# Attention and mixture of experts in one kernel: ranks in pieces, overflow tables among the second parts, late sign adds, sums and searches on VectorE

## The chip, the cores and the metric

The kernel runs on one core of one Trainium2 chip. A core has five engines with instruction streams of their own: TensorE (PE in the profile; PEld is its weight load), VectorE (DVE), ScalarE (ACT), GpSimd (POOL) and SyncE (SP, which here issues DMA transfers). Each works through its stream strictly in order and waits on semaphores for what other engines produce. The metric is the device time of one execution in microseconds (us).

## What is computed

Eight batches of eight heads attend over 576 tokens with 64 features a head; of each row of scores only the 32 largest are kept. The result, 4608 tokens of 512 features, goes through a mixture of eight experts, of which each token takes the one with the largest logit:

```python
scores = scale * np.matmul(q, k.transpose(0, 1, 3, 2))
kth = np.partition(scores, -top_k, axis=-1)[..., -top_k:-top_k + 1]
scores = np.where(scores >= kth, scores, -1000000000.0)
attn = softmax(scores); attn_out = np.matmul(attn, v)
...
logits = x @ w_gate
expert_idx = np.argmax(logits, axis=1)
for e in range(E):
    xe = x[expert_idx == e]
    h = np.maximum(xe @ w1[e], 0.0)
    out[expert_idx == e] = gate_w[expert_idx == e, None] * (h @ w2[e])
```

## The kernel before

**Attention.** A loop `for t in range(steps + LAG + TD + 2)` runs 144 steps and some trailing turns. A step handles two tiles of 128 queries by 576 keys. TensorE makes the scores (`scores`), ACT copies them to `sb`, VectorE searches the 32nd largest value of each row with MAX8 and MATCH_REPLACE (`topk`; its last entries make `nb`, the threshold). `softmax` lets ACT write the sign of score minus threshold to `sg`, and POOL adds it: `sb <- sb + sg`, so that what lies below the threshold falls far down. Then come nine transposes on TensorE (`transp`, tile `tt`), the Exp on ACT (`exps`, tile `et`) and the product with v (`av`, tile `px`). The softmax's two tiles are handled one after the other, and `nb` of the last tile waits in POOL's stream behind the first tile's add.

**Side jobs.** Besides these fixed lines there are generators, one for each kind of further work: `j_sums` (sums of the softmax), `j_rows` (scaling to `xm`, the logits), `j_find` (finds the rows where the number of values at the threshold isn't right, and writes keys `r_lw`, `r_key`), `j_redo` (does such rows again, with their own search over `r_sb`, and subtracts `r_wk` on POOL), `j_patch` (their Exp transposes, their product `r_xa`, stored to `xs`), `j_route` (positions `pos` in the table of tokens by expert; indirect writes to `table`). A job yields `need(pool=1.2, act=0.8)` and the like: what it wants to spend in this step. `advance` lets it go on if the step's budget holds; after the steps `drain` lets all of them go on by one piece for each MoE round, without a limit. What a job queues with `pe`, `act`, `vec`, `pool` is issued by `flush` at fixed places of the step.

**MoE.** `moe()` is a generator of 128 rounds k, each one eighth of an expert's features: `hidden(k)` (tile `ph`; ACT makes `hh`, VectorE the rest `hl`), `project(k - 1)` (tile `y`, from `hh`, `hl`), `load_w(k + 3)` on SP, `split_w(k + 2)` (each weight tile `r` is split into a high part `wh` and a low part `wl`, the second `wl` on POOL once no job is left, on VectorE before), and now and then `fetch` (load of `ids`, indirect gather `gx` of the tokens) and `turn_x` (transposes `mt`, high and low parts `xh`, `xl`). The first 64 rounds are first parts: 256 tokens of each expert, by number. The rounds from 64 on are second parts, where the experts are taken by the number of their tokens, so that unequal widths are compiled in. `j_ahead` gathers the first expert's tokens to `kt` while attention still runs.

**Ranks and overflow.** Which expert stands in which second part is known only from the counts of tokens. After the drain the program, in written order, takes `counts` from the histogram, checks `lost`, clears the ends of the `hh`/`hl` tiles, and calls `ranks` (VectorE: keys, a comparison of all with all, `rank`, `base`, and `rtab`, the table that SP reads for the second parts' weights and ids) and `over` (cumulated overflow tiles, `te` and `tr`, for experts with more tokens than the second parts hold). `over` calls `step()`, which runs one MoE round, between its pieces. The first second part's ids and weights are fetched from round 54 on, when `late["on"]` is there.

Of the kernel before, what the change touches and what calls it, by code (L numbers as in the profile page):

```python
# [8 lines left out]
F32 = mybir.dt.float32  # L9
F32R = mybir.dt.float32r  # L10
# [4 lines left out]
OP = mybir.AluOpType  # L15
# [16 lines left out]
LAG = 2  # L32
# [9 lines left out]
VALS = TOPK + EXTRA  # L42
T0 = V0 + VALS + 1
# [11 lines left out]
def attention_moe(ctx, tc, q, k, v, w_gate, w1, w2, out):  # L55
    nc = tc.nc
    B, H, S, D = q.shape
    HP = H // 2
    DM = H * D
    E = w_gate.shape[1]  # L60
# [6 lines left out]
    DC, FC = DM // 128, F // 128  # L67
# [65 lines left out]
    ones = consts.tile([128, 128], BF, name="ones")  # L133
# [39 lines left out]
    SG = []  # L173
# [111 lines left out]
    def need(**k):  # L285
        return k
# [142 lines left out]

    def topk(t, us):  # L430
# [26 lines left out]
        def second(i):  # L457
# [21 lines left out]
                  (nc.gpsimd.tensor_tensor, (nb, v[:, :, 0:T0 + 1:T0], factors, OP.mult)),  # L479
                  (nc.gpsimd.tensor_tensor, (nb[:, :, 1], nb[:, :, 1], after, OP.subtract))]  # L480
# [56 lines left out]
    def j_sums(n):  # L537
# [3 lines left out]
        b = n // 2  # L541
# [5 lines left out]
        pool(nc.gpsimd.tensor_tensor, both, both, nm.to_broadcast([128, 2, NT, 8 + VALS]), op=OP.add)  # L547
        pool(nc.gpsimd.tensor_scalar, w, nm, -1.0, shift(b)[:, 1:2], op0=OP.mult, op1=OP.add)
        pool(nc.gpsimd.tensor_scalar, w, w, -1.25 * FAR, 1.25 * FAR, op0=OP.max, op1=OP.min)
# [8 lines left out]
        pool(nc.gpsimd.tensor_tensor, sums, sums, less, op=OP.subtract)  # L558
        pool(nc.gpsimd.tensor_scalar, sums, sums, 1e-9, None, op0=OP.add)
        pool(nc.gpsimd.tensor_tensor, sums, sums, w, op=OP.mult)  # L560
# [196 lines left out]
    def j_redo(p):  # L757
# [28 lines left out]
        pool(nc.gpsimd.tensor_tensor, sb, sb, dr, op=OP.subtract)  # L786
        act(nc.scalar.activation, sb, sb, AF.Exp, bias=nb[:, 0:1], scale=0.125, accum_out=nb[:, 1:2])
        start("patch", j_patch(p, sb, nb, qi, hmb), 4 * NT * (p + 1) + DUE['patch'])

    def j_patch(p, ex, nb, qi, hmb):  # L790
# [27 lines left out]
        pool(nc.gpsimd.tensor_tensor, xa, xa, hmb, op=OP.mult)  # L818
# [256 lines left out]
    def j_ahead():  # L1075
# [209 lines left out]
    ring = [0]  # L1285
# [38 lines left out]
    def moe():  # L1324
# [11 lines left out]
        for k in range(NU * FC):  # L1336
            u, f = divmod(k, FC)
# [30 lines left out]
    def ranks(sb, counts):  # L1368
# [13 lines left out]
        nc.vector.tensor_reduce(base, both, axis=AX.X, op=OP.add)  # L1382
        nc.vector.tensor_tensor(both, more, eight[:, :, None].to_broadcast([128, E, E]), op=OP.mult)
# [5 lines left out]
    def over(sb, counts, base, otab, step=lambda: None):  # L1389
# [189 lines left out]
    pc = ps_a.tile([128, E], F32, name="mt")  # L1579
    lost = moe_a.tile([128, B], F32, name="lost")  # L1580
# [8 lines left out]
    late["h"] = [[late["sb"].tile([128, 512], F32R, name=f"{n}{i}") for n in ("hh", "hl")] for i in range(2)]
    for x in late["h"]:  # L1590
        for y in x:
            nc.vector.memset(y.bitcast(F32)[:, WIDE:], 0.0)
# [52 lines left out]
```

## Time and profile before

| | |
|---|---|
| median of 3 runs | 1209.81 us (1208.26 to 1212.22) |
| profiled execution, its own time | 1202.35 us |
| its span in the trace | 1200.5 us |
| mean granted clock of TensorE, of full speed | 0.985 |
| busy time PE / DVE / POOL / ACT | 1134.9 / 985.5 / 827.0 / 814.1 us |

Steps fill the trace up to about 690 us, first parts of the MoE run from 713 to about 930, second parts after that. How to read rows of the trace: start in us, duration in us, engine, line of the kernel, operation, out<-in by the program's names, size, and in square brackets the idle time of the engine before it with the engine, tile and line that ended it. An engine with short idle times near the span's length is the bound; of the others idle time is no loss.

### The profile page before, as it was taken

The numbers are of one execution on the slowest core, as the hardware profiler recorded it, in microseconds if no ns is written. First come the engines' busy times: TensorE is split into PE (matmuls) and PEld (weight loads), VectorE is DVE, ScalarE is ACT, GpSimd is POOL, SyncE is SP. The second block draws the span as 40 slices with busy tenths as digits, with TensorE's granted clock in tenths as the row PEclk, the third lists the DMA queues.
The fourth block names the chain that finished last, engine by engine and source line by source line (L and its number), as shares of the span: only waits on it lengthen the run. The fifth ranks groups of instructions, "written<-read, shape, count | busy, mean of one in ns | idle before, by whom it ended". The sixth has DMA issues, their size and how long they took to land. (4 is left out here: it accounts for less than half of the span.)

```text
span 1200.5 us, 32495 instructions
## 1 busy us (share of the span) xinstructions
PE 1134.9 (95%) x9444; PEld 886.7 (74%) x9444; DVE 985.5 (82%) x6586; ACT 814.1 (68%) x1668; POOL 827.0 (69%) x1378
## 2 busy tenths in 40 slices
PE   5899999999899999999999879899999999999997
PEld 2567777776667776676676668789878889988886
DVE  6999999999999999999999938758798444455554
ACT  3999999999989999889999743334333233323332
POOL 5788878896779888989888974533556455444644
PEclk8999999999999999999999989899999999999999
DMA  6756766676556666466664437667666555445763
GB/s 173 214 172 185 210 191 200 200 212 189 172 174 188 191 207 198 142 175 206 190 192 163 149 97 230 170 177 228 204 175 213 175 160 167 134 142 175 218 177 99
DMA packets 279754, 217.09 MB, mean 181 GB/s; under 512 B 135035, under 2 KB 221220, under 8 KB 279568
## 3 DMA queue, kind: packets, MB, share of 16 engines
q1 hardware_dynamic: 270432, 194.07, 54.4%
q0 software_dynamic: 7904, 20.58, 5.5%
q8 instruction: 76, 1.25, 0.5%
q14 instruction: 110, 0.90, 0.3%
q10 hardware_dynamic: 1232, 0.30, 0.1%
HBM read 108.69 MB, written 106.54 MB: 179 GB/s over the span
## 5 line engine op out<-in xcount | busy, mean ns | idle before, releaser
L1148 DVE MAX8 vq<-sb 128x8 f32<-128x48 f32 x3456 | 429.7, 199 | 3.3 <-ACT sb L382 3.3
L491 POOL TENSOR_TENSOR sb<-sb,sg 128x576 f32<-128x576 f32 x288 | 370.8, 1288 | 68.5 <-ACT sg L490 65.1
L511 PEld LDWEIGHTS px<-et,rv 128*64 128x64 f32 x3200 | 158.4, 137 | 117.7 <-ACT xt L273 36.4
L490 ACT ACTIVATE sg<-sb,nb 128x576 int8<-128x576 f32 x288 | 227.0, 788 | 19.0 <-POOL nb L1151 17.6
L1277 ACT ACTIVATE hh<-ph 128x256 fp32r<-128x256 f32 (+4 forms) x128 | 53.7, 420 | 230.7 <-PE ph L1276 188.0
L511 PE MATMUL px<-et,rv 128*64 128x128 f32 (+1 forms) x3200 | 191.3, 268 | 11.0 <-ACT xt L273 3.8
L1059 POOL TENSOR_TENSOR wl<-r,wh 128x512 fp32r<-128x512 f32 x82 | 107.9, 1318 | 128.2 <-DVE wh L1058 110.6
L497 PE MATMUL tt<-turner,sb 128*128 128x128 f32 x1296 | 176.0, 280 | 9.6 <-POOL sb L491 7.3
L501 ACT ACTIVATE et<-tt,shifts 128x1152 f32<-128x1152 f32 x144 | 177.9, 1236 | 5.6 <-PE tt L497 4.9
L380 PE MATMUL ps<-qk 64*128 64x512 f32 (+1 forms) x576 | 178.0, 645 | 3.1 <-ACT sb L382 2.5
L497 PEld LDWEIGHTS tt<-turner,sb 128*128 128x128 f32 x1296 | 139.2, 141 | 36.0 <-issue 17.1
L382 ACT ACTIVATE sb<-ps 128x1024 f32<-128x1024 f32 x144 | 148.4, 1030 | 25.3 <-PE ps L380 25.3
L1059 DVE TENSOR_TENSOR wl<-r,wh 128x512 fp32r<-128x512 f32 x170 | 132.8, 781 | 26.4 <-ACT wh L1056 22.3
L1276 PE MATMUL ph<-xh,wh 128*128 128x256 f32 (+4 forms) x480 | 149.9, 312 | 0.4 <-ACT xh L1262 0.4
L1283 DVE SCALAR_TENSOR_TENSOR hl<-ph,hh 128x256 fp32r<-128x256 f32 (+1 forms) x128 | 58.0, 453 | 112.0 <-ACT hh L1277 111.9
L1276 PE MATMUL ph<-xh,wl 128*128 128x256 f32 (+4 forms) x480 | 146.4, 305 | 0.4 <-DVE wl L1059 0.4
L1276 PE MATMUL ph<-xl,wh 128*128 128x256 f32 (+4 forms) x480 | 146.1, 304 | 0.0
L1303 PE MATMUL y<-wl,hh 128*128 128x512 f32 x316 | 125.6, 398 | 0.4 <-POOL spacer L1316 0.4
L1303 PE MATMUL y<-wh,hh 128*128 128x512 f32 x316 | 125.7, 398 | 0.0
L1159 DVE MAX8 vq<-vq 128x8 f32<-128x49 f32 (+1 forms) x576 | 120.0, 208 | 0.0
L1303 PE MATMUL y<-wh,hl 128*128 128x512 f32 x284 | 113.0, 398 | 3.8 <-DVE hl L1283 3.6
L1276 PEld LDWEIGHTS ph<-xh,wh 128*128 128x128 f32 x480 | 92.0, 192 | 7.2 <-ACT xh L1262 2.1
(285 smaller groups left out, 2079.0 us busy)
## 6 DMA issues: line engine op xcount, KB each, us to landing
r<-in_moe_w_dram SPq DMA_DIRECT2D x252, 256.0 KB
sc<-sb SPq DMA_DIRECT2D x128, 288.0 KB
sc<-sb SPq DMA_DIRECT2D x128, 256.0 KB
rv<-in_v_dram SPq DMA_DIRECT2D x32, 256.0 KB
xs<-xm SPq DMA_DIRECT2D x16, 512.0 KB
rq<-in_q_dram SPq DMA_DIRECT2D x60, 128.0 KB
rk<-in_k_dram SPq DMA_DIRECT2D x60, 128.0 KB
sc<-sb SPq DMA_DIRECT2D x32, 144.0 KB
```

What stands on the lines that cost most here:

```text
L380: nc.tensor.matmul(MAINS[:, n], qk[:, 0, w], qk[:, 1, 2 * LEFT:], start=True, stop=True)
L382: nc.scalar.activation(bass.AP(EX[-1].tensor, EX[-1].offset, [list(EX[-1].ap[0]), [S + LEFT, 2], [1, M]]), MAINS, AF.Copy)
L490: nc.scalar.activation(upper(SG[i]), SB[u], AF.Sign, bias=nb[:, i, 1:2], accum_out=CNT[b // 2][:, b % 2, 2 * lt + i:2 * lt + i + 1])
L491: return lambda: nc.gpsimd.tensor_tensor(SB[u], SB[u], SG[i], op=OP.add)
L497: nc.tensor.transpose(tt[:, c], x[:, c * 128:(c + 1) * 128], ident)
L501: nc.scalar.activation(ET[t], three.rearrange("p (c q) -> p c q", c=NB9), AF.Exp, bias=shift(t // (2 * NT))[:, 0:1], scale=0.125)
L511: yield lambda kb=kb, blk=blk: nc.tensor.matmul(px[h * 64:(h + 1) * 64], block(rv, p % 2, kb if kb < MAIN else MAIN + n, h), et[:, blk, q] ...
L1059: (nc.gpsimd if i and not any(lanes.values()) else nc.vector).tensor_tensor(lo, r, hi, op=OP.subtract)
L1148: one[m][0](*one[m][1])
L1159: f(*a)
L1276: nc.tensor.matmul(ph, a[:, c, :], x[:, c, 0:w], start=(m == 0), stop=(m == len(seq) - 1))
L1303: nc.tensor.matmul(PY[u, t], a[:, s], x, start=(f == 0 and m == 0), stop=(f == FC - 1 and m == len(seq) - 1))
```

## The change

- `spare(t)`: in the last two steps the adds of the signs and the last `nb` go to VectorE instead of POOL. So do the last `j_sums`, the last `j_find`, and, once the steps are done, `j_patch`'s multiply and sums of `r_xa`.
- `j_ahead` issues its two gathers together.
- `j_redo` yields once more between the subtract and the Exp after the steps.
- `ranks` gets a `step`, called three times, so that a MoE round runs between its pieces; the counts and the clears stand in rounds of their own, too.
- `lost` and `over` wait until `rounds[0]` has reached the second round group (`first * FC + FC`, round 72), and `over` gets a further `step()`.

```diff
+    def spare(t):
+        return nc.gpsimd if t < steps else nc.vector
...
-                  (nc.gpsimd.tensor_tensor, (nb, v[:, :, 0:T0 + 1:T0], factors, OP.mult)),
-                  (nc.gpsimd.tensor_tensor, (nb[:, :, 1], nb[:, :, 1], after, OP.subtract))]
+                  (spare(t + 1).tensor_tensor, (nb, v[:, :, 0:T0 + 1:T0], factors, OP.mult)),
+                  (spare(t + 1).tensor_tensor, (nb[:, :, 1], nb[:, :, 1], after, OP.subtract))]
...
-        return lambda: nc.gpsimd.tensor_tensor(SB[u], SB[u], SG[i], op=OP.add)
+        return lambda: spare(t + LAG).tensor_tensor(SB[u], SB[u], SG[i], op=OP.add)
...
-        pool(nc.gpsimd.tensor_tensor, both, both, nm.to_broadcast([128, 2, NT, 8 + VALS]), op=OP.add)
+        eng = nc.gpsimd if n < NQ - 1 else nc.vector
+        pool(eng.tensor_tensor, both, both, nm.to_broadcast([128, 2, NT, 8 + VALS]), op=OP.add)
...
         pool(nc.gpsimd.tensor_tensor, sb, sb, dr, op=OP.subtract)
+        if not att_open[0]:
+            yield
         act(nc.scalar.activation, sb, sb, AF.Exp, bias=nb[:, 0:1], scale=0.125, accum_out=nb[:, 1:2])
...
-        pool(nc.gpsimd.tensor_tensor, xa, xa, hmb, op=OP.mult)
+        pool((nc.gpsimd if in_steps[0] else nc.vector).tensor_tensor, xa, xa, hmb, op=OP.mult)
...
+        yield need(pool=2.2)
         for i in range(T):
-            yield need(pool=1.4)
             take(GX[0][i], ID[0][:, i, 0:1], c)
...
         for k in range(NU * FC):
+            rounds[0] = k
...
+        step()
         nc.vector.tensor_tensor(more, rank[:, :, None].to_broadcast([128, E, E]),
                                 eight[:, None, :].to_broadcast([128, E, E]), op=OP.is_equal)
         both = sb.tile([128, E, E], F32, name="both")
+        step()
...
+    nc.tensor.matmul(pc, ones, hist[:, :, KR], start=True, stop=True)
+    counts = moe_a.tile([128, E], F32, name="counts")
+    nc.vector.tensor_tensor(counts, pc, skip, op=OP.add)
+    next(g)
+    base = ranks(moe_a, counts, lambda: next(g))
+    next(g)
+    late["h"] = [[late["sb"].tile([128, 512], F32R, name=f"{n}{i}") for n in ("hh", "hl")] for i in range(2)]
+    for x in late["h"]:
+        for y in x:
+            nc.vector.memset(y.bitcast(F32)[:, WIDE:], 0.0)
+    late["on"] = True
+    while rounds[0] < first * FC + FC:
+        next(g)
     lost = moe_a.tile([128, B], F32, name="lost")
...
-    base = ranks(moe_a, counts)
     next(g)
-    late["on"] = True
     n = over(moe_a, counts, base, otab, lambda: next(g))
```

The order of instructions shows where this lands. POOL before, at the end of the steps (`sg_145` and `sg_147` are the signs of the two tiles of a step, `kt` the first gather of the MoE):

```order
L1151 TENSOR_TENSOR nb_280<-nb_280,nbt_276 128x2
L491 TENSOR_TENSOR sb<-sb,sg_147 128x576
L273 TENSOR_TENSOR vq_304<-vq_304,nb_280 128x18x47
L273 TENSOR_SCALAR vq_304<-nb_280,shifts 128x18
L273 TENSOR_SCALAR vq_304<-vq_304 128x18
L491 TENSOR_TENSOR sb<-sb,sg_145 128x576
L491 TENSOR_TENSOR sb<-sb,sg_147 128x576
L969 MEMSET spacer 1x1
L970 DMA kt<-xs,ids_13653 128x512
L273 TENSOR_SCALAR r_lw<-nb_279,shifts 128x36
```

POOL after, at the same place:

```order
L273 TENSOR_TENSOR r_xa<-r_xa,r_hm 128x512
L976 MEMSET spacer 1x1
L977 DMA kt<-xs,ids_13653 128x512
L976 MEMSET spacer 1x1
L977 DMA kt<-xs,ids_13653 128x512
L850 MEMSET spacer 1x1
L851 DMA lps<-r_lr,r_qi 37888x8
```

VectorE after, at the end of the steps:

```order
L494 TENSOR_TENSOR sb<-sb,sg_145 128x576
L449 TENSOR_REDUCE vq_304<-mid 128x2x8
L1158 TENSOR_REDUCE vq_304<-vq_304 128x2x9
L1158 TENSOR_REDUCE vq_304<-vq_304 128x2
L1158 TENSOR_TENSOR nb_280<-vq_304,factors 128x4
L1158 TENSOR_TENSOR nb_280<-nb_280,nbt_276 128x2
L494 TENSOR_TENSOR sb<-sb,sg_147 128x576
L273 RECIPROCAL rinv<-sums 128x2x4 x2
L273 RECIPROCAL rinvl<-sums 128x2
L273 TENSOR_TENSOR vq_304<-vq_304,nb_280 128x18x47
```

The last four adds, the last `nb` pair and the adjustment of the last sums have left POOL and stand on VectorE in one piece; both `kt` gathers follow each other on POOL.

POOL before, in the rounds of the redo, up to the subtract of `r_sb`:

```order
L927 DMA table<-pay,pos 36864x4
L969 MEMSET spacer 1x1
L970 DMA gx<-xs,ids_13659 128x512
L926 MEMSET spacer 1x1
L927 DMA table<-pay,pos 36864x4
L926 MEMSET spacer 1x1
L927 DMA table<-pay,pos 36864x4
L273 TENSOR_TENSOR r_sb<-r_sb,r_wk 128x576
```

POOL after, at that place:

```order
L977 DMA gx<-xs,ids_13659 128x512
L933 MEMSET spacer 1x1
L934 DMA table<-pay,pos 36864x4
L933 MEMSET spacer 1x1
L934 DMA table<-pay,pos 36864x4
L933 MEMSET spacer 1x1
L934 DMA table<-pay,pos 36864x4
L933 MEMSET spacer 1x1
L934 DMA table<-pay,pos 36864x4
L273 TENSOR_TENSOR r_sb<-r_sb,r_wk 128x576
```

Two more of the eight `table` writes of the last route stand ahead of the subtract (the two first ones stand above the rows shown in both kernels).

VectorE before, right after the drain (`hl` at the end is that of the next round):

```order
L1374 SCALAR_TENSOR_TENSOR key<-counts,edesc 128x8
L1375 TENSOR_TENSOR more<-key 128x64
L1377 TENSOR_REDUCE rank<-more 128x8
L1378 TENSOR_TENSOR more<-rank,eight 128x64
L1381 TENSOR_TENSOR both<-more,caps 128x64
L1382 TENSOR_REDUCE base<-both 128x8
L1383 TENSOR_TENSOR both<-more,eight 128x64
L1384 TENSOR_REDUCE of<-both 128x8
L1385 CAST rtab<-of 128x8
L1386 TENSOR_SCALAR rtab<-of 128x8
L1283 SCALAR_TENSOR_TENSOR hl<-ph,hh 128x256
```

VectorE after, at the same place of the program:

```order
L1594 TENSOR_TENSOR counts<-mt,skip 128x8
L1290 SCALAR_TENSOR_TENSOR hl<-ph,hh 128x256
L1066 TENSOR_TENSOR wl_16081<-r_16024,wh_16080 128x512
L1065 CAST wh_16082<-r_16025 128x512
L1382 SCALAR_TENSOR_TENSOR key<-counts,edesc 128x8
L1383 TENSOR_TENSOR more<-key 128x64
L1385 TENSOR_REDUCE rank<-more 128x8
L1290 SCALAR_TENSOR_TENSOR hl<-ph,hh 128x256
L1066 TENSOR_TENSOR wl_16136<-r_16076,wh_16135 128x512
L1065 CAST wh_16137<-r_16077 128x512
L1387 TENSOR_TENSOR more<-rank,eight 128x64
L1290 SCALAR_TENSOR_TENSOR hl<-ph,hh 128x256
```

What stood in one round before is now divided by the `hl`, `wl` and `wh` of a round each.

## Rows read from the trace of the kernel before

**Rows 1.** The page: span, then busy time of each engine, its share and instructions.

```profile
span 1200.5 us, 32495 instructions
...
PE 1134.9 (95%) x9444; PEld 886.7 (74%) x9444; DVE 985.5 (82%) x6586; ACT 814.1 (68%) x1668; POOL 827.0 (69%) x1378
```

**Rows 2.** Windows: length, busy PE, PEld, DVE, ACT, POOL, clock, DMA share, GB/s.

```profile
686.00:712.95 26.95, 18.85 (x204) 15.27 (x201) 9.16 (x34) 14.96 (x30) 24.31 (x38) 0.94 0.28 69
750.13:760.42 10.29, 9.18 (x52) 7.84 (x51) 9.96 (x27) 2.04 (x5) 2.49 (x7) 0.83 0.70 198
769.39:780.72 11.33, 7.86 (x43) 6.84 (x41) 4.78 (x11) 4.10 (x9) 9.76 (x18) 0.85 0.65 166
865.11:885.85 20.74, 17.15 (x101) 14.82 (x99) 18.68 (x60) 5.89 (x12) 11.14 (x16) 0.92 0.61 152
885.85:904.54 18.69, 18.36 (x118) 15.85 (x116) 18.52 (x38) 7.83 (x16) 10.53 (x11) 1.00 0.71 210
904.54:907.36 2.82, 2.82 (x20) 2.56 (x18) 2.79 (x12) 0.90 (x2) 0.82 (x2) 1.00 0.05 10
913.00:920.85 7.85, 7.03 (x38) 5.14 (x36) 5.77 (x7) 1.92 (x4) 6.98 (x8) 1.00 0.96 313
978.59:1013.57 34.98, 34.98 (x182) 31.59 (x180) 18.21 (x29) 12.11 (x23) 17.97 (x20) 1.00 0.55 163
```

**Rows 3.** Timeline of TensorE at the transition (start, duration, operation, [idle before, releaser]).

```profile
692.88 1.31 PE L511 MATMUL px<-et,rv 128*64 128x128 f32 x20 [0.36 <-ACT xt L273]
695.85 0.66 PE L497 MATMUL tt<-turner,sb 128*128 128x128 f32 x4 [1.65 <-POOL sb L491]
697.51 1.18 PE L497 MATMUL tt<-turner,sb 128*128 128x128 f32 x5 [1.00 <-POOL sb L491]
```

**Rows 4.** Timeline of ACT there: the last two signs.

```profile
690.51 0.78 ACT L490 ACTIVATE sg<-sb,nb 128x576 int8<-128x576 f32 x1 [0.73 <-POOL nb L1151]
...
696.25 0.78 ACT L490 ACTIVATE sg<-sb,nb 128x576 int8<-128x576 f32 x1 [2.31 <-POOL nb L1151]
```

**Rows 5.** Timeline of POOL there: the last add but one.

```profile
694.52 1.27 POOL L491 TENSOR_TENSOR sb<-sb,sg 128x576 f32<-128x576 f32 x1
```

**Rows 6.** Timeline of VectorE around the transition.

```profile
688.98 0.20 DVE L273 TENSOR_TENSOR lp<-pt,rinv 128x48 f32<-128x48 f32 x1
...
700.40 1.25 DVE L1059 TENSOR_TENSOR rv<-rq,rv 128x512 fp32r<-128x512 f32 x1 [11.22 <-ACT rv L1056]
...
704.87 0.69 DVE L1059 TENSOR_TENSOR rv<-rk,rv 128x512 fp32r<-128x512 f32 x1 [1.06 <-ACT rv L1056]
```

**Rows 7.** Timeline of TensorE: round 10, and the transposes of the redo.

```profile
753.30 0.50 PE L1303 MATMUL y<-wh,hl 128*128 128x512 f32 x1 [1.11 <-DVE hl L1283]
...
775.84 0.59 PE L273 MATMUL pt<-turner,r_sb 128*128 128x128 f32 x3 [3.47 <-ACT r_sb L273]
```

**Rows 8.** Timeline of VectorE: the first pair of the redo's search.

```profile
746.33 0.76 DVE L273 MAX8 r_v<-r_sb 128x8 f32<-128x576 f32 x1
...
747.20 0.74 DVE L273 MATCH_REPLACE8 r_wk<-r_v,r_sb 128x576 f32<-128x576 f32 x1
```

**Rows 9.** Timeline of POOL: the first of six indirect issues, and the subtract behind them.

```profile
765.85 1.05 POOL L927 DMA_INDIRECT table<-pay,pos  x1 [4.87 <-DVE pos L273]
...
773.60 1.29 POOL L273 TENSOR_TENSOR r_sb<-r_sb,r_wk 128x576 f32<-128x576 f32 x1
```

**Rows 10.** Timeline of ACT: the redo's Exp.

```profile
774.92 0.77 ACT L273 ACTIVATE r_sb<-r_sb,r_nb 128x576 f32<-128x576 f32 x1 [5.81 <-POOL spacer L926]
```

**Rows 11.** Timeline of TensorE: the longer wait at the ranks.

```profile
880.45 0.50 PE L1303 MATMUL y<-wh,hl 128*128 128x512 f32 x1 [2.18 <-DVE hl L1283]
```

**Rows 12.** Timeline of VectorE: an add of the overflow tables.

```profile
884.78 2.04 DVE L1413 TENSOR_TENSOR te<-te,tmp 128x44 f32<-128x44 f32 x1
```

**Rows 13.** Timeline of POOL beside it.

```profile
885.44 1.31 POOL L1059 TENSOR_TENSOR wl<-r,wh 128x512 fp32r<-128x512 f32 x1
```

**Rows 14.** Timeline of SP: the ids of the first second part.

```profile
908.44 0.35 SPq L1235 DMA_DIRECT2D ids<-table  x1
```

**Rows 15.** Timeline of POOL ahead of that transfer.

```profile
907.03 1.29 POOL L1059 TENSOR_TENSOR wl<-r,wh 128x512 fp32r<-128x512 f32 x1 [2.00 <-DVE wh L1058]
```

More of the change, by code (lines that the diff above doesn't have):

```diff
@@ L546, in j_sums @@
         w = both[:, :, :, 7:8]
-        pool(nc.gpsimd.tensor_tensor, both, both, nm.to_broadcast([128, 2, NT, 8 + VALS]), op=OP.add)
-        pool(nc.gpsimd.tensor_scalar, w, nm, -1.0, shift(b)[:, 1:2], op0=OP.mult, op1=OP.add)
-        pool(nc.gpsimd.tensor_scalar, w, w, -1.25 * FAR, 1.25 * FAR, op0=OP.max, op1=OP.min)
+        eng = nc.gpsimd if n < NQ - 1 else nc.vector
+        pool(eng.tensor_tensor, both, both, nm.to_broadcast([128, 2, NT, 8 + VALS]), op=OP.add)
+        pool(eng.tensor_scalar, w, nm, -1.0, shift(b)[:, 1:2], op0=OP.mult, op1=OP.add)
+        pool(eng.tensor_scalar, w, w, -1.25 * FAR, 1.25 * FAR, op0=OP.max, op1=OP.min)
         yield need(act=0.8)
@@ L557, in j_sums @@
         yield need(pool=0.8)
-        pool(nc.gpsimd.tensor_tensor, sums, sums, less, op=OP.subtract)
-        pool(nc.gpsimd.tensor_scalar, sums, sums, 1e-9, None, op0=OP.add)
-        pool(nc.gpsimd.tensor_tensor, sums, sums, w, op=OP.mult)
+        pool(eng.tensor_tensor, sums, sums, less, op=OP.subtract)
+        pool(eng.tensor_scalar, sums, sums, 1e-9, None, op0=OP.add)
+        pool(eng.tensor_tensor, sums, sums, w, op=OP.mult)
         yield need(slack=1)
@@ L679, in j_find @@
         lw = sm("r_lw", [128, 2, NLT])
+        eng = nc.gpsimd if p < B // 2 - 1 else nc.vector
         for j in range(2):
             b = 2 * p + j
-            pool(nc.gpsimd.tensor_scalar, lw[:, j], NBB[b % 4][:, :, 0], shift(b)[:, 3:4], BIG, op0=OP.is_gt, op1=OP.mult)
-        pool(nc.gpsimd.tensor_tensor, lw, CNT[p], lw, op=OP.add)
+            pool(eng.tensor_scalar, lw[:, j], NBB[b % 4][:, :, 0], shift(b)[:, 3:4], BIG, op0=OP.is_gt, op1=OP.mult)
+        pool(eng.tensor_tensor, lw, CNT[p], lw, op=OP.add)
         key = sm("r_key", [128, 2, NLT])
-        pool(nc.gpsimd.tensor_scalar, key, lw, float(2 * TOPK - S), 1.0, op0=OP.is_equal, op1=OP.subtract)
-        pool(nc.gpsimd.tensor_tensor, key, key, below1.rearrange("p (j x) -> p j x", j=2), op=OP.mult)
+        pool(eng.tensor_scalar, key, lw, float(2 * TOPK - S), 1.0, op0=OP.is_equal, op1=OP.subtract)
+        pool(eng.tensor_tensor, key, key, below1.rearrange("p (j x) -> p j x", j=2), op=OP.mult)
         yield need(slack=1)
@@ L835, in j_patch @@
         while w:
-            pool(nc.gpsimd.tensor_tensor, xa[:, 0:w], xa[:, 0:w], xa[:, w:2 * w], op=OP.add)
+            pool((nc.gpsimd if in_steps[0] else nc.vector).tensor_tensor, xa[:, 0:w], xa[:, 0:w], xa[:, w:2 * w], op=OP.add)
             w //= 2
@@ L1283, in hidden @@
             nc.vector.scalar_tensor_tensor(to, ph[:, c], 0.0, hh[:, c], op0=OP.max, op1=OP.subtract)
-    ring = [0]
+    ring, rounds = [0], [0]
     def y_bank(u):
@@ L1366, in attention_moe, with ranks @@
     rtab = consts.tile([128, 2, E], I32, name="rtab")
-    def ranks(sb, counts):
+    def ranks(sb, counts, step):
         key = sb.tile([128, E], F32, name="key")
@@ L1380, in ranks @@
         both = sb.tile([128, E, E], F32, name="both")
+        step()
         nc.vector.tensor_tensor(both, more, caps[:, None, :].to_broadcast([128, E, E]), op=OP.mult)
         nc.vector.tensor_reduce(base, both, axis=AX.X, op=OP.add)
+        step()
         nc.vector.tensor_tensor(both, more, eight[:, :, None].to_broadcast([128, E, E]), op=OP.mult)
@@ L1399, in over @@
         nc.vector.tensor_copy(ov, ovi)
+        step()
         for e in range(E):
@@ L1584, in attention_moe @@
     nc.vector.tensor_reduce(lost1[:, 0:1], lost, axis=AX.X, op=OP.add)
-    nc.tensor.matmul(pc, ones, hist[:, :, KR], start=True, stop=True)
-    counts = moe_a.tile([128, E], F32, name="counts")
-    nc.vector.tensor_tensor(counts, pc, skip, op=OP.add)
     nc.vector.tensor_scalar(lost1[:, 0:1], lost1[:, 0:1], 1.0, None, op0=OP.min)
[L1589 to L1592, printed above, removed]
-    base = ranks(moe_a, counts)
     next(g)
-    late["on"] = True
     n = over(moe_a, counts, base, otab, lambda: next(g))
```

## The prediction

> **What bounds the kernel now.** I began with the busy times of the page: TensorE (PE) is busy 1134.9 us, 95% of the span, and no other engine passes 82% [rows 1]. So a change that adds no matmul can win only what TensorE loses: the 65 us in which it idles, and the stretches in which its granted clock lies at the lower of its two levels (1.2 instead of 2.4 GHz). I then listed TensorE's gaps over the whole span and looked at those near code that the change touches. Windows around them show length, busy time and clock [rows 2]. The reader should see five places:
>
> - The transition from the loop of steps to MoE (686 to 712.95): TensorE is busy 18.85 of 26.95 us, clock 0.94, GpSimd (POOL) 24.31.
> - MoE rounds 10 and 11 (750.13 to 760.42): 10.29 us, 9.18 busy, clock 0.83, VectorE (DVE) 9.96.
> - Four rounds around the redo transposes (769.39 to 780.72): 7.86 busy of 11.33, clock 0.85, POOL 9.76.
> - The five rounds at the ranks (865.11 to 885.85): 17.15 busy of 20.74, clock 0.92, DVE 18.68.
> - Two rounds at 913 to 920.85: 7.85 us, and the DMA engines 96% busy.
>
> One undisturbed round of a first part (904.54 to 907.36) takes 2.82 us. That is my yardstick for a round. A low clock costs its window (1 - clock) x length; for rounds 10 and 11 that is 0.17 x 10.29 = 1.75 us, and for the ranks 0.08 x 20.74 = 1.66.
>
> The single rows of these places say who ends each wait; they come below with the term that they carry. The profiled execution took 1202.35 us against a median of 1209.81, 0.6% less. The terms are worked out in the profiled execution and taken off the median. 0.3% of the median, 3.6 us, is about what a measurement of this kernel can tell from no change.
>
> **Part A, the last signs and sums on VectorE.** At the transition TensorE waits 1.65 and then 1.00 us ahead of the sign transposes `tt`, both released by POOL's add `sb<-sb,sg` [rows 3]. The reason stands one engine earlier: ACT's last sign waits 2.31 us for POOL's `nb` [rows 4], which is queued behind the previous add, 1.27 us on POOL from 694.52 [rows 5], though the sign it adds ended at 690.51 + 0.78 = 691.29. VectorE meanwhile idles for 11.22 us up to 700.40 [rows 6]. The change puts the adds, the reduces and `nb` of the last two steps on VectorE. The trace has no such add there; it lies between 0.20 (128x48) and 1.25 us (a 128x512 with POOL at work), and nearest is the 128x512 of 0.69 [rows 6], by size 0.78. Then the first add ends near 692.1, `nb` a microsecond later, the second add near 694.7 with ACT's sign of 0.78 between. TensorE's own work before `tt` ends at 692.88 + 1.31 = 694.19, so both waits go except for a few tenths: 2.65 us. The second group of five transposes takes 1.18 us where the first of four takes 0.66 [rows 3]; at the first's rate it would be 0.83, another 0.35. **A = 3.0.** Lower bound 1: the four adds now stand ahead of the scalings `xm` and `lp` on VectorE, and TensorE meets the next wait sooner. Upper bound 5: the window idles 26.95 - 18.85 = 8.1 us in all, and the kt gathers, now issued together ahead of the sums, could free some of the rest.
>
> **Part B, the search one round later.** One more yield in the redo moves the first MAX8 and MATCH_REPLACE, 0.76 and 0.74 us [rows 8], by one round. In round 10 TensorE waits 1.11 us for `hl` of VectorE [rows 7], which is busy for 9.96 of the window's 10.29. With 1.5 us less ahead of it, `hl` is in time: 1.11 won, and the low clock of 1.75 us that follows this wait, 2.86 together. VectorE's total up to the end of the search is unchanged, and two rounds later a pair stands where a single MAX8 stood. A part comes back there, estimated 0.4, a quarter of the pair, since VectorE has so little to give. 2.86 - 0.4 = 2.46.
>
> **Part C, the redo transposes two rounds later.** TensorE waits 3.47 us for ACT's `r_sb` [rows 7]; ACT's Exp at 774.92 [rows 10] waits for POOL's subtract, which ran at 773.60 [rows 9]. POOL had six indirect issues between 765.85 and 773.60, so (773.60 - 765.85) / 6 = 1.29 us each. Two rounds are 5.64 us more for this chain, but two further `table` issues now stand ahead of the subtract, so it comes 2.6 us later at an unchanged start; TensorE also comes 2.5 us earlier by B. The wait becomes 3.47 - 5.64 + 2.6 + 2.5 = 2.9, hence a gain of 0.5. The clock loss here (0.15 x 11.33 = 1.7) follows such a wait and stays. **B + C = 3.0**, bounds 1 (B given back entirely) and 5 (C's clock comes back too).
>
> **Part D, ranks in pieces.** Now all of counts, lost, ranks and memsets stand on VectorE in one round, followed by the overflow table a piece per round. TensorE idles 20.74 - 17.15 = 3.59 us here, of which 2.18 is one wait for `hl` [rows 11], and loses 1.66 to the clock; the next rounds up to 904.54 idle 18.69 - 18.36 = 0.33 [rows 2]. Sum 5.58. After the change two to four of these small operations stand in a round, and the overflow tables run in second parts. A window of those (978.59 to 1013.57) has TensorE busy for all 34.98 us with VectorE at 18.21: 16.8 us are free, and the overflow's operations are put there at nothing. If that cover were gone, they would cost about what the rounds now lose, 0.33 plus part of D. **D = 5.6**, bounds 5.0 (residual waits of 0.1 per round) and 6.6 (later rounds gain what `hl` lateness leaves behind).
>
> Against this stands a row: a VectorE add of 128x44 took 2.04 us [rows 12], where a 128x48 took 0.20 [rows 6]. POOL's `wl`, 1.31 us at 885.44, ran in that time [rows 13]. So the pieces could each cost ten times their size. I weigh it lightly, because the rounds that hold most such pieces before lost only 0.33 us in 18.69. The Trainium skill (SBUF — State Buffer, section "Who interferes with whom") says that a VectorE instruction with two SBUF inputs and a GpSimd instruction that reads SBUF exclude each other for a whole instruction; the row agrees. By that rule each piece with two inputs could stand still for a `wl`, which is the rival "held up" below.
>
> **Part F, the stall after the ranks.** The queue of SP holds the weight loads. Its `ids` transfer went at 908.44 [rows 14], right behind a POOL operation queued after the `wl` of 907.03, which had waited 2.00 us for VectorE [rows 15]. VectorE was late from the overflow pieces. The weights came in one burst, and the rounds at 913 took 7.85 us instead of 2 x 2.82 = 5.64: 2.2 lost. Without the pieces VectorE is on time. **F = 1.5**, bounds 0 (POOL is late by itself) and 2.5.
>
> Sum: 3.0 + 3.0 + 5.6 + 1.5 = 13.1 us. From 1202.35 that is 1189.25 for a profile, from the median **1196.7**. Its own range: the lower bounds of A to F sum to 7.0 and the upper to 19.1; they will not all fall on one side, so 1191 to 1202.
>
> **Rivals.**
> - *VectorE becomes the bound where the work lands.* For: during the search and after the ranks VectorE is busy 97 and 99% of a window [rows 2], and the late multiplies of the redo go there too. Then A and B come out near 1 each, F at 0, D at 5: gain 7, 1202.8. Against: in the undisturbed rounds TensorE doesn't wait for it. Chance 0.2.
> - *The edits around redo and transition do nothing*, because ACT and the longer POOL chain of issues set the end anyway (two rounds more, but also two issues more). Only D is left, less some waiting: gain 5.3, 1204.5. Chance 0.1.
> - *Held up:* the pieces stand still behind POOL. The overflow has some 26 operations with two inputs. Each held for 2.04 - 0.20 = 1.84 us makes 48 us, against 16.8 free: 31 lost, less the gain of 13, 1227.9. It decides from a mean hold of (16.8 + 13.1) / 26 = 1.15 us; between 0.65 and that it only eats the gain. Against: POOL is busy in half of that window. Chance 0.05 of slower; 0.04 of eating the gain to nothing.
>
> **How the numbers follow.** The likeliest case has 0.61. Its time, 1196.7, is the forecast. Faster by over 0.3%: 0.61 + 0.2 + most of the second rival's 0.1 = 0.89; same: 0.06; slower: 0.05. The range reaches from 1189 (upper bounds of all terms, 19.1 off, is 1190.7; 1.7 more for the medians, since three runs of before lie 4 us apart) to 1205 (the second rival).
>
> **What the profile would show.** Right: no wait for POOL's `sb` ahead of the last `tt`, and hidden(0) 3 us earlier; no `hl` wait in rounds 10 and 11; a wait for `r_sb` of about 3 us still there; no wait above 0.3 us in rounds 44 to 52 and a clock of 1.00; `ids` issued right behind the `table` load with no wait for the iota; second-part rounds unchanged. Wrong: if TensorE waits for `xm`/`lp` transposes or for `xt` as long as it waited for `sb`, A fails; if a new `hl` wait of over 1 us stands where a search pair or a late fold went, B fails; a rank operation of over 1 us beside a TensorE wait would show the hold.

## The result and the profile after

The changed kernel takes 1197.94 us in the median of 7 runs (1196.31 to 1204.77), the kernel before beside it 1209.59 (1208.07 to 1214.07). The ratio is 0.9914 with a 95% interval of 0.9897 to 0.993, so 10.4 us less (8.5 to 12.5); the ratio weighs all runs, the medians alone lie 11.7 us apart. Two later comparisons gave 0.9899 (0.9884 to 0.9914) and 0.9905 (0.9882 to 0.9927). The kernel before ran at 1203 to 1212 us on the chips used, so only ratios of one comparison are set against each other.

I took a second trace of both kernels, because the two first ones are not a pair. The trace of [rows 1] came out 7 us under the runs timed beside it, and the first trace of the changed kernel has ScalarE waits that the second one lacks (last section). The second pair is 1204.22 us before and 1193.67 after. Its two traces come from different chips too; the last of the windows below, rounds with nothing to gain, lasts 47.63 and 47.62 us on them. Windows of the kernel before in this pair, columns as in [rows 2]: transition (from the products ahead of the last `tt` but one to hidden(0)), rounds 10 and 11, rounds 12 to 14, rounds 15 to 25, the five rounds at the ranks, the nine after them, the five with the weight burst, eleven second-part rounds.

```profile
693.04:715.89 22.85, 16.64 (x141) 13.96 (x141) 7.60 (x20) 9.55 (x17) 20.31 (x31) 0.78 0.36 99
753.09:761.89 8.80, 7.70 (x53) 6.46 (x51) 8.60 (x24) 2.04 (x5) 1.47 (x3) 1.00 0.67 199
761.89:771.12 9.23, 9.18 (x61) 8.07 (x60) 8.77 (x19) 4.70 (x10) 4.32 (x9) 1.00 0.69 190
771.12:816.71 45.59, 41.16 (x265) 34.36 (x263) 25.68 (x49) 16.74 (x37) 24.52 (x44) 0.96 0.62 170
867.77:888.48 20.71, 17.14 (x100) 14.94 (x99) 18.64 (x60) 5.67 (x12) 11.11 (x16) 0.92 0.65 154
888.48:915.61 27.13, 26.81 (x171) 23.53 (x170) 24.01 (x52) 11.60 (x24) 15.90 (x17) 1.00 0.59 178
915.61:932.90 17.29, 16.54 (x103) 14.03 (x102) 15.20 (x22) 6.58 (x13) 11.85 (x12) 1.00 0.90 280
980.51:1028.14 47.63, 47.63 (x245) 43.01 (x244) 24.84 (x39) 16.55 (x31) 24.75 (x27) 1.00 0.56 171
```

The same eight stretches of the changed kernel, second trace:

```profile
694.85:714.74 19.89, 13.96 (x141) 11.72 (x141) 12.98 (x35) 9.10 (x17) 8.00 (x14) 0.91 0.37 99
752.27:759.93 7.66, 7.66 (x53) 6.46 (x51) 7.49 (x19) 2.04 (x5) 2.55 (x6) 1.00 0.71 218
759.93:769.98 10.05, 9.19 (x62) 8.07 (x61) 9.84 (x22) 4.32 (x10) 2.46 (x5) 1.00 0.56 168
769.98:813.02 43.04, 41.08 (x264) 34.22 (x263) 26.81 (x53) 17.16 (x37) 18.81 (x33) 0.96 0.72 187
864.18:879.27 15.09, 15.09 (x100) 13.52 (x99) 11.00 (x24) 5.67 (x12) 12.29 (x21) 1.00 0.77 161
879.27:905.52 26.25, 26.25 (x171) 23.82 (x170) 17.93 (x38) 11.59 (x24) 16.75 (x19) 1.00 0.71 223
905.52:921.29 15.77, 15.58 (x103) 13.93 (x102) 12.71 (x21) 6.69 (x13) 10.26 (x9) 1.00 0.93 272
968.93:1016.55 47.62, 47.62 (x244) 43.01 (x243) 37.62 (x90) 16.53 (x31) 24.67 (x27) 1.00 0.58 171
```

The first number behind a window is its length. Row by row the changed kernel wins 2.96, 1.14, -0.82, 2.55, 5.62, 0.88, 1.52 and 0.01 us, 13.9 in all. The span is only 10.9 shorter; 1.81 of the other 3.0 were lost ahead of the first window, which begins that much later in the changed kernel's trace. At the ranks TensorE is now busy for all 15.09 us at full clock. In the second parts VectorE works 12.8 us more, and TensorE loses nothing. At the transition the clock is 0.91 instead of 0.78, though TensorE is idle about as long (5.93 and 6.21 us): of the 2.96 won there, 2.68 is busy time at a higher clock.

TensorE's waits there in the changed kernel, second trace, answering [rows 3]:

```profile
694.85 1.31 PE L514 MATMUL px<-et,rv 128*64 128x128 f32 x20 [0.36 <-ACT xt L273]
696.09 0.66 PE L500 MATMUL tt<-turner,sb 128*128 128x128 f32 x4
697.68 0.77 PE L500 MATMUL tt<-turner,sb 128*128 128x128 f32 x5 [0.94 <-DVE sb L494]
...
701.43 1.00 PE L273 MATMUL pt<-turner,xt 128*128 128x144 f32 x6 [2.65 <-DVE lp L273]
```

VectorE, answering [rows 6]:

```profile
693.37 0.91 DVE L494 TENSOR_TENSOR sb<-sb,sg 128x576 f32<-128x576 f32 x1 [5.15 <-ACT sg L493]
...
695.12 1.83 DVE L1158 TENSOR_TENSOR nb<-nb,nbt 128x2 f32<-128x2 f32 x1
696.88 0.75 DVE L494 TENSOR_TENSOR sb<-sb,sg 128x576 f32<-128x576 f32 x1
...
699.36 1.43 DVE L494 TENSOR_TENSOR sb<-sb,sg 128x576 f32<-128x576 f32 x2
700.71 0.55 DVE L273 TENSOR_TENSOR xm<-pt,rinv 128x384 f32<-128x384 f32 x1
701.18 0.20 DVE L273 TENSOR_TENSOR lp<-pt,rinv 128x48 f32<-128x48 f32 x1
```

And GpSimd beside that `nb`:

```profile
694.77 1.07 POOL L934 DMA_INDIRECT table<-pay,pos  x1 [0.17 <-issue]
695.88 1.05 POOL L273 TENSOR_TENSOR r_xa<-r_xa,r_hm 128x512 f32<-128x512 f32 x1
```

The reader should see three things. The wait of 1.65 for the first add is gone. One of 0.94 stays: the second add stands on VectorE behind a tiny `nb` of 1.83 us, and TensorE goes on when that add ends. And a new one of 2.65 stands where `xm` and `lp` come behind the adds.

### The profile page after: what moved, and what is told of

Its sections match the earlier page's. It is cut to its first block, busy times and chain, and to the rows that moved or that the text cites. A ratio compares the mean times of both kernels' runs of the same rounds, so it can differ in the third digit from the quotient of the medians.

```text
span 1195.6 us, 32489 instructions
## 1 busy us (share of the span) xinstructions
PE 1130.6 (95%) x9444; PEld 884.0 (74%) x9444; DVE 989.9 (83%) x6612; ACT 813.6 (68%) x1668; POOL 805.7 (67%) x1352
## 5 line engine op out<-in xcount | busy, mean ns | idle before, releaser
L494 POOL TENSOR_TENSOR sb<-sb,sg 128x576 f32<-128x576 f32 x284 | 364.6, 1284 | 71.6 <-ACT sg L493 68.3
L1066 POOL TENSOR_TENSOR wl<-r,wh 128x512 fp32r<-128x512 f32 x80 | 105.2, 1316 | 121.5 <-DVE wh L1065 97.2
L1066 DVE TENSOR_TENSOR wl<-r,wh 128x512 fp32r<-128x512 f32 x172 | 133.7, 777 | 28.5 <-ACT wh L1063 12.8
```

The source lines that it names most:

```text
L494: return lambda: spare(t + LAG).tensor_tensor(SB[u], SB[u], SG[i], op=OP.add)
L1066: (nc.gpsimd if i and not any(lanes.values()) else nc.vector).tensor_tensor(lo, r, hi, op=OP.subtract)
```

## Experiments

**The three parts alone**, each as an edit of the kernel before. The ranks and the overflow (the hunks from `ranks` to the end of the diff):

```diff
-    def ranks(sb, counts):
+    def ranks(sb, counts, step):
...
+    while rounds[0] < first * FC + FC:
+        next(g)
```

> The kernel before with one part of the change: ranks and overflow in pieces, overflow among the second parts. By the prediction's sum (D 5.6 and F 1.5) this alone is worth 7.1 us, a ratio of 0.994. The rival, that the two small-operation rounds only make way for waits elsewhere (the traces of before and of the changed kernel differ by 5.5 us from round 43 on), gives 5.5 us or 0.9955. If pieces stood still behind GpSimd and cost TensorE time, it would be 1.000 or more. In the profile: no wait for hl at the ranks, second-part rounds of 4.21 us as before.

Measured: 1196.71 against 1203.31 us, ratio 0.9939 (0.9923 to 0.9955), so 7.3 us. In its trace the five rounds at the ranks take 16.66 us instead of 20.71. Only one wait there is left, 1.41 us for `xl` ahead of the histogram's matmul, which the kernel before has too. The five rounds with the burst take 15.85:

```profile
867.17:883.83 16.66, 15.25 (x101) 13.68 (x100) 10.31 (x25) 5.69 (x12) 11.72 (x16) 1.00 0.78 197
...
910.29:926.14 15.85, 15.65 (x104) 13.99 (x102) 13.79 (x21) 6.69 (x13) 10.45 (x10) 1.00 0.91 267
```

The late adds, `nb`, sums, find, redo multiplies and the gathers of `kt`:

```diff
+    def spare(t):
+        return nc.gpsimd if t < steps else nc.vector
...
+        yield need(pool=2.2)
```

> The kernel before with one other part: last sign adds, nb, sums, find and redo multiplies on VectorE, kt gathers together. By the prediction A is worth 3.0 us, ratio 0.9975. The rival, read from the changed kernel's trace: the wait for the adds becomes a wait of 2.65 us for lp, which now stands behind the adds on VectorE, so it is worth 0 (1.000), or loses up to 1.6 us (1.0013), which hidden(0) came later there. In the profile: where hidden(0) starts, counted from the last but one group of products with v; 20.1 us in before.

Measured: 1200.92 against 1203.31, ratio 0.9982 (0.9972 to 0.9991), 2.2 us. Its trace has the wait of 2.65 for `lp`, and rounds 10 and 11 take 7.65 us: the wait for `hl` that I had put down to the redo's yield goes with this part. The search does start one round later here, 36.3 us behind hidden(0) (713.89) instead of 33.4; with the yield alone it is 33.6 (hidden(0) at 718.11). Its first MAX8 in the second trace of before, with this part and with the yield alone:

```profile
749.30 0.75 DVE L273 MAX8 r_v<-r_sb 128x8 f32<-128x576 f32 x1
750.21 0.75 DVE L273 MAX8 r_v<-r_sb 128x8 f32<-128x576 f32 x1
751.70 0.75 DVE L273 MAX8 r_v<-r_sb 128x8 f32<-128x576 f32 x1
```

Rounds 12 to 14 take 10.04 instead of 9.23, so 0.8 of the 1.1 comes back. Rounds 15 to 25 take 46.79 instead of 45.59, so 1.2 is lost: eight indirect issues instead of six stand ahead of the redo's subtract here, and TensorE, whose transposes come one round later, waits 4.79 us for `r_sb`. The two further issues belong to this part, not to the yield. The waits in the second trace of before and with this part:

```profile
778.53 0.90 PE L273 MATMUL pt<-turner,r_sb 128*128 128x128 f32 x3 [4.43 <-ACT r_sb L273]
778.99 0.90 PE L273 MATMUL pt<-turner,r_sb 128*128 128x128 f32 x3 [4.79 <-ACT r_sb L273]
```

The redo's yield:

```diff
         pool(nc.gpsimd.tensor_tensor, sb, sb, dr, op=OP.subtract)
+        if not att_open[0]:
+            yield
```

> The kernel before with the one extra yield of the redo. By the prediction B and C are worth 3.0 us (ratio 0.9975), nearly all from the hl wait in round 10 and its low clock. The rival, read from the changed kernel's trace: the hl wait stays at 0.8 us, and what is won is the low clock after the wait for r_sb, 1.4 us (0.9988). If the yield does nothing by itself, 1.000.

Measured: 1198.48 against 1203.31, ratio 0.9954 (0.9939 to 0.997), 5.5 us, beyond both theories. TensorE in round 10 and at the redo:

```profile
758.67 0.50 PE L1305 MATMUL y<-wh,hl 128*128 128x512 f32 x1 [1.10 <-DVE hl L1285]
...
780.95 0.44 PE L273 MATMUL pt<-turner,r_sb 128*128 128x128 f32 x2 [1.62 <-ACT r_sb L273]
```

The wait for `hl` stands as before: the new yield stands in the job behind the search and can't move it. The wait for `r_sb` is 1.62 us, in the second trace of before 4.43, and no low clock follows it. The transposes come one round later (2.82 us by the prediction's yardstick), still with six issues ahead of the subtract: 4.43 - 2.82 = 1.61. Rounds 15 to 25 take 41.26 us against 45.59, so this trace shows 4.3 of the 5.5; rounds 43 to 61 give another 1.6.

**The kernel before once more:**

> The kernel before, unchanged, for a second trace and for what the comparison calls no change: a ratio of 1.000 within about 0.002. The first profiled execution was 7 us faster than the median of its timed runs. If that was chance, this trace shows some of the 7 us: more low clock episodes or longer waits than the first one at the same places. If the profiled execution is always that much faster, its span is again near 1200 while the timed runs are near 1209.

Ratio 1.000 (0.9988 to 1.0011). Its profiled execution took 1204.22 us where its timed ones took 1203.11: being profiled didn't make it faster.

**The changed kernel once more:**

> The changed kernel, unchanged, for a second trace. If the gains of the three parts measured alone add up (7.3 + 2.2 + 5.5 us), it is 15.0 us faster, ratio 0.9875. If they overlap, as the first comparison had it, 10 us, 0.9914. The first trace shows waits of 2.7 to 4 us of ScalarE for signals of TensorE (hidden(0), round 45) that no row of the kernel explains, and has 8% fewer semaphore records than the others: if they belong to that one execution, they are not here, and rounds 43 to 56 are some 4 us shorter than in the kernel before by 10 instead of 3.4 us; if they belong to the program, they stand at the same places.

1193.55 against 1206.11 us, ratio 0.9899 (0.9884 to 0.9914), 12.2 us. The unexplained waits aren't in this trace, and rounds 43 to 56 win 6.5 us (5.62 + 0.88). The three parts alone add up to 15.0; their intervals are 1 to 2 us wide on either side each, so an overlap of 2.8 isn't shown by the times. The traces show about 1 us of it: rounds 43 to 61 are 6.2 us shorter with the ranks and the overflow alone, but also 1.3 with the late jobs and 1.6 with the yield, though neither edit is made there; together 9.1, and 8.0 in the changed kernel.

The second `ids` still waits for the iota in this trace. Two rows of SP, then two of GpSimd:

```profile
894.56 0.36 SPq L1240 DMA_DIRECT2D ids<-table  x1
899.32 0.35 SPq L1242 DMA_DIRECT2D ids<-table  x1
```

```profile
897.92 1.29 POOL L1066 TENSOR_TENSOR wl<-r,wh 128x512 fp32r<-128x512 f32 x1 [1.95 <-DVE wh L1065]
899.16 0.14 POOL L1239 IOTA ids<- 128x4 int32 x1
```

The second goes 4.76 us behind the first, in the second trace of before 5.08 (905.97 and 911.05), and the `wl` ahead of the iota has waited 1.95 us for VectorE, as in [rows 15].

**`nb` without GpSimd beside it**, an edit of the changed kernel:

```diff
-        pool((nc.gpsimd if in_steps[0] else nc.vector).tensor_tensor, xa, xa, hmb, op=OP.mult)
+        pool((nc.gpsimd if p < B // 2 - 2 else nc.vector).tensor_tensor, xa, xa, hmb, op=OP.mult)
```

> The changed kernel with one operation moved: the multiply of r_xa at the end of the steps runs on VectorE ahead of the adds instead of on GpSimd. In the changed kernel VectorE's nb of 128x2 took 1.83 us there and ended 0.03 us after GpSimd's multiply of 1.05 us. If the two exclude each other, nb falls to about 0.2 us, ScalarE's next sign no longer waits 1.14 us, TensorE's wait of 0.94 us ahead of tt is gone, and hidden(0) comes up to 1.6 us earlier: ratio 0.0013 below that of the changed kernel. If nb was slow for a reason of its own (a late input), it stays at 1.8 us and the time doesn't change.

Ratio 0.9855 (0.9839 to 0.9872) against 0.9899 of the changed kernel in the same comparison, 5.3 us. VectorE and GpSimd in its trace:

```profile
690.33 2.19 DVE L273 TENSOR_TENSOR r_xa<-r_xa,r_hm 128x512 f32<-128x512 f32 x1 [3.56 <-ACT r_xa L273]
...
695.52 0.16 DVE L1158 TENSOR_TENSOR nb<-nb,nbt 128x2 f32<-128x2 f32 x1
```

```profile
690.66 1.29 POOL L494 TENSOR_TENSOR sb<-sb,sg 128x576 f32<-128x576 f32 x1
691.91 0.66 POOL L1158 TENSOR_TENSOR nb<-vq,factors 128x4 f32<-128x4 f32 x1
```

`nb` falls from 1.83 to 0.16 us, and the nine `tt` follow one another without a wait. The hold has moved: the multiply itself takes 2.19 us beside GpSimd's add, and GpSimd's own `nb` 0.66 instead of 0.20 behind it; TensorE's wait for the add of the step before grows from 0.64 to 1.46. From the products to hidden(0) this trace takes 21.21 us, 1.32 more than the changed kernel's: less waiting, but a lower clock.

```profile
695.25:716.46 21.21, 16.71 (x140) 14.12 (x140) 11.35 (x35) 8.98 (x17) 8.13 (x17) 0.76 0.45 128
```

So the hold is shown, but not that its going shortens the transition. The time fell by more than the 1.6 us expected; the trace, at 1193.37 the slowest of its four runs, doesn't show where from.

**The redo's subtract on VectorE**, an edit of the changed kernel:

```diff
-        pool(nc.gpsimd.tensor_tensor, sb, sb, dr, op=OP.subtract)
+        (pool if in_steps[0] else vec)((nc.gpsimd if in_steps[0] else nc.vector).tensor_tensor, sb, sb, dr, op=OP.subtract)
```

> The changed kernel with the redo's subtract after the steps on VectorE, so that it doesn't stand behind eight indirect issues on GpSimd. If these issues are what TensorE still waits for, through ScalarE's Exp, the wait ahead of the transposes of r_sb (1.6 us with the yield alone) is gone and the kernel is about 1.5 us faster than the changed one, ratio lower by 0.0012. If the chain is bound elsewhere (search, ScalarE's turn), the wait stays and so does the time; if the subtract delays hl, a wait for hl of up to 0.8 us takes its place.

Ratio 0.9854 (0.9834 to 0.9875), 5.4 us below the changed kernel. The wait of 1.96 us, here as the changed kernel's second trace has it, is gone, with the low clock that followed it:

```profile
780.56 0.55 PE L273 MATMUL pt<-turner,r_sb 128*128 128x128 f32 x3 [1.96 <-ACT r_sb L273]
```

From round 15 to 42 this kernel has TensorE busy for all 90.50 us at full clock, where the changed one took 94.20 with 92.24 busy at 0.98: 3.7 of the 5.4 us, against 1.5 expected. First this kernel, then the changed one:

```profile
769.88:860.38 90.50, 90.50 (x597) 79.23 (x596) 66.62 (x135) 38.57 (x83) 37.10 (x67) 1.00 0.74 213
```

```profile
769.98:864.18 94.20, 92.24 (x597) 80.52 (x596) 66.73 (x134) 38.45 (x83) 37.76 (x68) 0.98 0.72 204
```

**The scalings ahead of the last two adds**, an edit of the changed kernel:

```diff
-            softmax(t - LAG, grp(t - LAG), 0)()
...
+        if t < steps:
+            first_add()
         flush(pq)
+        if t >= steps:
+            flush(dq)
+            first_add()
```

> The changed kernel with the scalings xm and lp of the last rows ahead of the last two adds on VectorE instead of behind them. If TensorE's 2.65 us wait for lp is made by the adds' place, it shrinks by the two adds, 1.34 us, to 1.3 us, and the ratio falls by 0.0011; the adds come 0.75 us later, which tt of that step can bear. If TensorE then waits for the adds instead, nothing is won.

Ratio 0.9867 (0.9849 to 0.9885), 3.9 us below the changed kernel where 1.3 was expected; the two intervals touch. The wait for `lp` shrinks from 2.65 to 0.93 us. A second one of 0.67, for the `lp` that follows, takes part of it, and a lower clock the rest: the transition lasts 19.83 us, 19.89 in the changed kernel.

```profile
692.74:712.57 19.83, 15.16 (x140) 12.78 (x141) 12.87 (x32) 9.12 (x17) 9.24 (x18) 0.83 0.48 136
```

So the three single edits came out at three to four times what was expected of them, and only the redo's trace shows a gain at the place of the edit. Where the rest comes from stays open.

**All three edits:**

> The changed kernel with the three edits together that each took a wait away: the r_xa multiply on VectorE ahead of the adds, xm and lp ahead of the last two adds, the redo's subtract on VectorE. The waits named so far are 0.94 us (tt), 2.65 us (lp, 2.17 and 0.93 us with one edit) and 1.96 us (r_sb), so with all three up to 5.5 us of waiting can go, plus 1.7 us for a low clock episode that followed the wait for r_sb: a ratio of 0.984 to 0.985 against the kernel before. The rival: they share what they win, since a shorter wait for lp brings TensorE earlier to the gathers kt, and the ratio is that of the best single one, 0.9855.

On the next chip it gave 0.9921 (0.9893 to 0.995) beside 0.9905 for the changed kernel. The named waits are gone or below 0.5 us, and the transition takes 17.59 us, 2.3 less than in the changed kernel's second trace. But ScalarE stalls like those of the first trace of the changed kernel are there, longer ones among them. So it ran once more:

> The kernel with the three edits together, once more. Its first trace shows stalls of 3 to 4.7 us in which ScalarE waits for signals of TensorE (hidden(0), 783, round 45) that the traces of the single edits don't have, and 8% fewer semaphore records. If those stalls belong to the chip of that run, the waits of the three places are gone here and nothing takes their place: ratio 0.983 to 0.985. If they belong to the kernel, they stand at the same places and the ratio is again 0.992.

0.9894 (0.9875 to 0.9912), and the stalls are there again: TensorE waits 7.28 us at 780 for ScalarE, which waits 9.87. By what I wrote they belong to the kernel; but the changed kernel alone has stalls of this kind on two comparisons and lacks them on a third, and neither run of all three was on that chip. Every trace of one comparison is alike in this, so the stalls go with the comparison rather than with the edit. Whether the three edits together beat the single ones is open.

**The overflow back in first parts**, and the changed kernel beside it:

```diff
-    while rounds[0] < first * FC + FC:
-        next(g)
```

> The changed kernel with lost and over not kept for the second parts but right behind the ranks, a piece per round as in the kernel before. This parts D from F. By the prediction's terms the weights' stall around round 57 comes back (F, 1.5 us, up to 2.2) and waits of 0.3 to 1 us in the rounds of the pieces: a ratio 0.0015 to 0.0025 above that of the changed kernel, 0.992. The rival: ranks in pieces alone were what mattered, VectorE has room for over in first parts too, and the ratio stays that of the changed kernel, 0.990.

> The changed kernel, unchanged, on the chip of the two others, to set them against: 0.990 as in its second comparison, within 0.0015.

0.9936 (0.9916 to 0.9957) against 0.9905 (0.9882 to 0.9927). The difference is 3.8 us, more than the 1.8 to 3.0 expected; the intervals overlap, and the profiled executions, 1207.03 and 1200.95, lie 6.1 apart. The traces show where: 1.8 us in rounds 48 to 56 (28.02 against 26.25) and 4.5 in rounds 57 to 61, first with the overflow early, then in the changed kernel of the same comparison:

```profile
914.47:934.84 20.37, 17.85 (x104) 15.19 (x102) 19.57 (x42) 6.48 (x14) 11.98 (x12) 0.92 0.79 242
```

```profile
912.67:928.55 15.88, 15.68 (x104) 14.00 (x102) 13.72 (x22) 6.79 (x14) 10.12 (x9) 1.00 0.90 268
```

In the first, one operation on VectorE, an indirect issue and two `wl` on GpSimd, and TensorE's wait behind them:

```profile
918.60 3.21 DVE L1424 TENSOR_SCALAR tmp<-tl_i,cum 128x44 f32<-128x44 f32 x1
```

```profile
918.08 1.13 POOL L1324 DMA_INDIRECT out_dram<-yo,ids  x1 [0.21 <-issue]
919.24 2.52 POOL L1066 TENSOR_TENSOR wl<-r,wh 128x512 fp32r<-128x512 f32 x2
```

```profile
922.62 0.56 PE L1310 MATMUL y<-wh,hl 128*128 128x512 f32 x1 [1.52 <-DVE hl L1290]
```

A compare of 128x44 that takes 0.24 us alone took 3.21, up to the end of the second `wl` (921.81 and 921.76), and `hl` behind it came late.

## Why the prediction was right, step by step

The forecast of 13.1 us less met 10.4 to 12.2, and the range held. The terms fared unequally: D carried the sum by the mechanism forecast, the others had a step wrong, and that they came near their sum is luck in part.

- **A, 3.0 forecast.** Mis-sized, with a step that failed: "both waits go except for a few tenths". `nb` was held up beside GpSimd (0.94 left), and the lower bound's mechanism, `xm` and `lp` behind the adds, cost 2.65, as much as the two waits for `sb` before. By the sign written down for it, A failed. From the products at the start of the window to the `xt` transposes the changed kernel takes 6.58 us, before 6.24 and 5.55: nothing won there. What the windows give, 2.96, is a shorter low clock, and the second trace of before has two further waits for `sb` (0.98 and 0.76) that the first lacks. Against the first trace, 20.07 us from 692.88 to 712.95, it is 0.2. The part alone, with the B that belongs to it, measured 2.2.
- **B, 2.46 forecast for the redo's yield.** The step that failed is "one more yield in the redo moves the first MAX8 and MATCH_REPLACE": the yield stands behind the search, and alone it leaves the wait. The late jobs on VectorE move the search by a round, and then `hl` is in time, as forecast. They win 1.1 in rounds 10 and 11 and return 0.8 in 12 to 14 (0.4 forecast, as a wait for `xl`, 0.86). The low clock behind that wait wasn't in the second trace of before.
- **C, 0.5 forecast.** Two rounds and two further issues are right for the whole change: the late jobs bring one round and the issues, the yield the other round. Mis-sized was the wait left, 2.9 forecast and 1.96 measured. Counted from hidden(0) in the second traces, TensorE comes 5.65 us later and the subtract 3.17: 4.43 - 5.65 + 3.17 = 1.95. The 2.5 us that B was to bring aren't there, and the wait started from 4.43 instead of 3.47. The low clock that I left in place stayed. Rounds 15 to 25 won 2.55. B + C was 1.14 - 0.82 + 2.55 = 2.87 against 3.0: the sum held by two errors that cancel.
- **D, 5.6.** Right in mechanism: in the changed kernel's second trace no wait and no low clock is left at the ranks. In size D and F can only be taken together, 7.1 forecast: 7.3 measured alone, 6.2 in that trace and 8.0 in the changed kernel's second one. Not all of the 8.0 is D's: with the late jobs or the yield alone the five rounds take 18.91 and 18.37 us instead of 20.71, at full clock, though a wait for `hl` of 1.98 and 1.42 stays. And in the two traces of the changed kernel that have the ScalarE stalls these rounds take 18.28 and 19.72.
- **F, 1.5.** Right in size, 1.52, but the step "without the pieces VectorE is on time" failed. GpSimd's `wl` still waited 1.95 us for VectorE, and the second `ids` went 4.76 us behind the first instead of 5.08, where the forecast had no such wait. What shortened rounds 57 to 61 is open; that the overflow's place matters there, the run with the overflow early shows.
- **The overflow in second parts at nothing.** Right: 0.01 us. In first parts it cost 3.8 by the comparison, with overlapping intervals, and more in the traces.
- **Rivals.** The operations do stand still behind GpSimd, but in the eleven rounds of the second parts only some five with two inputs, for 1 to 1.7 us each, and two with one input, for 1.0 and 1.1: 8.4 of the 22.8 us that VectorE had free there. "Held up" needed a mean of 1.15 over 26. "VectorE becomes the bound" came true where work landed at the transition (the wait for `lp`) and in rounds 12 to 14 (the wait for `xl`): it gave B near 1 us, and B won 0.3. For D and F it didn't come true.

## What to carry to other kernels

Work moved to an idle engine takes its place in that engine's order: look at what is queued behind it and who waits for that, as much as at what it no longer waits for. Small VectorE operations in rounds without slack can cost what GpSimd does beside them, not their own size; put them where the engine has the time of a whole GpSimd operation to spare. And when two terms of a forecast share an input, as B and C did, a single edit alone tells them apart where the sum doesn't. A wait that goes is worth time only where the stretch gets shorter: two edits at the transition took waits away and got a lower clock for it.

## What the hardware showed that I had not expected

VectorE operations can last as long as what GpSimd does beside them, also with little data: 0.16 to 1.83 us for 128x2, 0.24 to 3.21 for 128x44, 0.69 (another operation) to 2.19 for 128x512, each ending within 0.6 us of a GpSimd operation's end. These three began while GpSimd was issuing an indirect transfer (the compare at 918.60, the issue from 918.08 to 919.21) and lasted to the end of elementwise work behind it. So did all five that took over 1.3 us more than usual after 700 us in the changed kernel's second trace; over a hundred others that began during such an issue did not. The 128x44 compare has only one tensor among its inputs. The Trainium skill (SBUF — State Buffer, section "Who interferes with whom") lists `tensor_scalar` among the operations that can take both ports and says that issue order, not shape, decides who blocks. The trace agrees with the first; the second it leaves open, since the compare's record begins 0.64 us ahead of the first `wl`'s and the compare was the one held.

In some comparisons ScalarE waits for TensorE's signal long after TensorE's rows end. In the first trace of the changed kernel `kt`'s transposes end at 710.74, and the copy behind them starts at 713.42:

```profile
713.42 1.08 ACT L273 ACTIVATE rv<-ps 128x512 fp32r<-128x512 f32 x2 [6.16 <-remote]
```

```profile
709.65 1.09 PE L273 MATMUL ps<-turner,kt 128*128 128x128 f32 x8
714.56 0.58 PE L1283 MATMUL ph<-rv,rv 128*128 128x256 f32 x1 [3.81 <-ACT rv L273]
```

It shows in five traces, at hidden(0), around rounds 17 to 20 and at round 45, not at every place in each, mostly in stretches where GpSimd issues one indirect transfer after another; all five hold 8% fewer semaphore records than the others (24,724 to 24,766 against 26,926 to 26,978). The changed kernel has them in two comparisons and lacks them in a third, so the order of the kernel alone doesn't make them. Both traces of the kernel before have the full number of records and no such stall. Whether the chip or the recording makes it, and whether the kernel before would stall there too, stays open.
